# Sliding-window attention and a mixture of experts: the last expert's tiles fetch and turn the next tiles' x as all others do

## The chip, the cores and the metric

The kernel runs on one core of one Trainium2 chip. A core has TensorE (PE in the profile; its weight loads are listed as PEld), VectorE (DVE), ScalarE (ACT), GpSimd (POOL) and SyncE (SP), and 16 DMA engines which move data between HBM and the on-chip memory (SBUF, 128 partitions). TensorE writes its results to PSUM, which is divided into banks. The metric is the device time of one execution in microseconds; of several runs the median is given.

## The reference

What is computed are two layers, one after the other. The first is causal attention over a sliding window of 64 positions, for 8 batches, 8 heads, 576 positions and heads of 64. Its result is 4608 tokens of 512 numbers. The second is a mixture of 8 experts in which every token goes to one expert:

```python
logits = x @ w_gate                      # 4608 x 8
expert_idx = np.argmax(logits, axis=1)
probs = softmax(logits); gate_w = probs[token, expert_idx]
for e in range(E):                       # E = 8; the tokens of expert e
    h = np.maximum(x_sorted[lo:hi] @ w1[e], 0.0)      # 512 -> 1024
    y_sorted[lo:hi] = h @ w2[e]                       # 1024 -> 512
out = gate_w[:, None] * y                # back in the order of the tokens
```

How many tokens an expert gets depends on the data. With the reference's inputs the numbers are 669, 400, 748, 505, 592, 390, 566 and 738 for the experts 0 to 7. Everything is float32.

## The kernel before, in words

The first part of the program computes attention and the gate logits, scales every token by its gate weight and stores it as a row of x_dram in HBM (4608 rows, and row 4608, which holds zeros). Two tiles of expert 0 are begun here already. This takes a little over 300 us of the profile and the change doesn't touch its code.

The second part works on **tiles** of 256 slots (TB = 256, in C = 2 halves of 128). The experts' tiles are numbered one after the other; a table perm_i gives for each slot the token in it, or 4608 if the slot is empty. It has a column of 128 slots for each half tile, with columns for two halves ahead of tile 0, so that `slots(a)` in the tile numbered t is the tile t - 1 + a: `slots(0)` is the tile before, and `slots(3)` the second tile after t. The numbers run on from one expert to the next, and past the last tile the table holds empty slots only.

A tile is computed by body (L479). In order of the program it does this:

- finish() (L425) adds up the last part of the tile before, on DVE, and scatter (L291) writes that tile's rows to the output with two indirect DMAs issued from POOL.
- Where the tile is full, hidden (L336) computes h = relu(x w1) and output (L393) computes h w2. Both use a product with seven block multiplications in place of eight, so that sums and differences of blocks have to be formed: of the weights on POOL, of x and of the results on DVE. The order of all instructions on each engine is the order in which the program gives them.
- While TensorE works on this tile, the next tile's x is made ready. Its 256 rows lie in xg. turned_blocks (L310) turns them into xn with 16 DVE instructions, which are called in small groups between the other DVE work of the tile (`some(blocks, n)`); keep_turned (L325) copies xn to xq on ACT; sums_x (L329) forms four differences on DVE. The last two stand in output between the third and the fourth of its block products.
- When xg has been turned, gather (L272) fetches the x of the second tile after into xg: a small copy of the offsets and two indirect DMAs of 128 rows each, all on POOL.

If no more than 160 slots of an expert's last tile are used, half_tile (L436) computes it instead of hidden and output, in the plain form; it turns, gathers and sums in the same way.

The tiles of an expert are run by expert (L1063), one and more (L1070 to L1090). The numbers of tiles are known only when the kernel runs, so more nests branches: for each n up to KT - 1 = 2 there is one piece of code for a full tile and one for a half tile. All that is written once for each expert, since the weights' buffers change with e (w1s[e % 2] and so on, loaded by SP one expert ahead). If an expert has more than KT = 3 tiles, any_number (L1092) runs instead of all this; it is a loop over tiles without any overlap. It needs a small table, tiles_of.

In the last expert, one leaves something out. The lines are these:

```python
ends = e == E - 1 and (n == KT - 1 or not full)
body(e, slots(0), None if ends or e == E - 1 and n == KT - 2 else slots(3), full, between, not ends)
```

The third argument of body is what to gather (None: nothing), and the last one, next_x, says whether the next tile's x is turned and summed. With ends, that is in the third tile of the last expert and in any half tile of it, neither is done. In its second tile, if it is full, x is turned but nothing is gathered. After the last tile the code at L1126 and L1127 runs finish() and scatter() once more.

Of the kernel before, what the change touches and what calls it, by code (L numbers as in the profile page):

```python
# [11 lines left out]
F32 = mybir.dt.float32  # L12
# [3 lines left out]
ALU = mybir.AluOpType  # L16
AX = mybir.AxisListType
# [7 lines left out]
def _ins(ap: bass.AP, axis: int, n: int) -> bass.AP:  # L25

    dims = [list(d) for d in ap.ap]
    dims.insert(axis, [0, n])
    return bass.AP(tensor=ap.tensor, offset=ap.offset, ap=dims)


def _inner(ap: bass.AP, n: int) -> bass.AP:
    return _ins(ap, len(ap.ap), n)
# [3 lines left out]
def kernel(  # L37
# [11 lines left out]
    P = nc.NUM_PARTITIONS  # L49
    B, H, S, D = q.shape  # L50
    NT, DM = out.shape
    E = moe_w_gate.shape[1]
# [15 lines left out]
    NTILE = (NT + TB - 1) // TB + E - 1 + NE  # L68
    NX = NTILE + 4
    NS = NX * C  # L70
    KT = 3
# [24 lines left out]
    expert_i = consts.tile([P, NTILE], I32, name="expert_i")  # L96
# [4 lines left out]
    V, G = nc.vector, nc.gpsimd  # L101
# [48 lines left out]
    def sums_w1(e):  # L150
        form(left_sums(G, s1s[e % NW], *w1q(e)))
# [4 lines left out]
    def load_w1(e):  # L156
        return nc.sync.dma_start(out=w1s[e % NW][:], in_=w1v[e])
# [10 lines left out]
    lane = consts.tile([P, P], BF16, name="lane")  # L168
# [9 lines left out]
    with tc.tile_pool(name="tmp", bufs=1) as tmp:  # L178
# [8 lines left out]
        for i in range(BG):  # L187
# [12 lines left out]
            out=before[:], in_=ones[:], pattern=[[1, P]], compare_op=ALU.is_gt, fill=0.0, base=0,  # L200
# [6 lines left out]
    nt, cum, start, chunk0 = (consts.tile([P, E], F32, name=n) for n in ("nt", "cum", "start", "chunk0"))  # L207
    rt = ctx.enter_context(tc.tile_pool(name="rt", bufs=1))
# [31 lines left out]
    v_m = Memory(consts.tile([P, 3 * 2 * BG * NV * 2 * VW], F32, name="v_m"))  # L240
# [27 lines left out]
    def form_all(parts):  # L268
        for _ in parts:
            pass  # L270
# [20 lines left out]
    def scatter(tokens):  # L291
        G.tensor_copy(out=at_s[:], in_=tokens)
        for c in reversed(range(C)):

            put = G.indirect_dma_start(  # L295
                out=out[:, :], out_offset=bass.IndirectOffsetOnAxis(ap=at_s[:, c : c + 1], axis=0),
                in_=ys[c], in_offset=None, bounds_check=NT - 1, oob_is_err=False,
            )
            tc.declare_no_dep(put.ins, group="puts", reason="every token has one slot, so no row is written twice")
            tc.add_to_no_dep_group("puts", put.ins)  # L300
# [9 lines left out]
    def turned_blocks():  # L310

        rows = xg_all.rearrange("p c (g b j) -> p c g b j", b=P // QD, j=QD)
        for a in range(P // QD):
            for b in range(P // QD):
                V.transpose(  # L315
                    out=xn[b * QD : (b + 1) * QD, :, :, a * QD : (a + 1) * QD].rearrange("p c g i -> p (c g) i"),
                    in_=rows[a * QD : (a + 1) * QD, :, :, b, :].rearrange("p c g j -> p (c g) j"),
                )
                yield
# [73 lines left out]
    def output(e, blocks=None, next_x=True):  # L393

        b11, b12, b21, b22 = w2q(e)
        t = s2s[e % NW]
        a11, a12, a21, a22 = hq[:, 0, 0], hq[:, 1, 0], hq[:, 0, 1], hq[:, 1, 1]
        form(left_sums(V, hs, a11, a12, a21, a22))
        if blocks is not None:
            form_all(blocks)  # L400
        product_y(yx, a11, b11)
        nc.scalar.copy(out=y1, in_=yx)
        yield
        product_y(yw, a22, t[:, 3])
        yield
        product_y(yx, a12, b21, start=False)
        if blocks is None:
            sums_x(tps)
        elif next_x:
            keep_turned()  # L410
            sums_x([xn[:, c] for c in range(C)])
        yield
        product_y(yy, hs[:, 1], t[:, 1])
        yield
        product_y(yy2, hs[:, 2], t[:, 2])
        plus(v1, yy, y1)
        plus(v3, yy2, v1)
        V.tensor_tensor(out=ys[1][:, lo_], in0=v3, in1=yw, op=ALU.subtract)
        yield
        product_y(yw2, hs[:, 0], t[:, 0])  # L420
        yield
        product_y(yx2, hs[:, 3], b22)
        yield

    def finish():  # L425

        plus(ys[1][:, hi_], yw2, v3)
        plus(v2, yw2, v1)
        plus(ys[0], yps[0], v02)
# [49 lines left out]
    def body(e, last, after, full, between=None, next_x=True):  # L479

        finish()
        scatter(perm_i[:, last])
        if between is not None:
            between()
        blocks = turned_blocks() if next_x else iter(())
        if not full:
            half_tile(e, blocks, after, next_x)
            return
        form_all(hidden(e, blocks))
        parts = output(e, blocks, next_x)  # L490
        next(parts)
        if after is not None:
            gather(perm_i[:, after])
        form_all(parts)
# [559 lines left out]
    with tc.manual_schedule():  # L1054
        load_w1(1)
        load_w2(1)
        def at(n):
            n = nc.s_assert_within(
                n, 0, NTILE - 1, skip_runtime_bounds_check_because="a tile with a token is one of the NTILE"
            )  # L1060
            return lambda ahead: bass.ds((n + ahead) * C, C)

        def expert(e):  # L1063

            fulls, tiles, first = regs[e]
            if 0 < e < E - 1:
                load_w1(e + 1)
                load_w2(e + 1)

            def one(n, full, between=None):  # L1070
                slots = at(first + n)
                ends = e == E - 1 and (n == KT - 1 or not full)
                body(e, slots(0), None if ends or e == E - 1 and n == KT - 2 else slots(3), full, between, not ends)

            def more(n, between=None):

                with tc.If(tiles > n) as some_left:  # L1077
                    with tc.If(fulls > n, preferred_fallthrough_block=False) as full:
                        one(n, True, between)
                        if n + 1 < KT:  # L1080
                            more(n + 1)
                    with full.Else():
                        one(n, False, between)
                if between is not None:
                    with some_left.Else():
                        between()

            if e:
                one(0, True, partial(sums_w2, e))
            more(1 if e else NE, partial(sums_w1, e + 1) if e + 1 < E else None)  # L1090

        def any_number():  # L1092

            tiles_of = rt.tile([P, E, NTILE], F32, name="tiles_of")
            V.tensor_tensor(
                out=tiles_of[:], in0=_inner(cum[:], NTILE), in1=_ins(lane[:, 0:NTILE], 1, E), op=ALU.is_le
            )
            with nc.allow_low_precision("integers"):
                V.tensor_reduce(out=expert_i[:], in_=tiles_of[:].rearrange("p e t -> p t e"), axis=AX.X, op=ALU.add)
            _, (tiles,) = nc.values_load_multi_w_load_instructions(  # L1100
                places_i[0:1, E : E + 1], min_val=0, max_val=NTILE,
                skip_runtime_bounds_check_because="a sum of numbers of tiles, at most NTILE for any tokens",
            )
            with tc.For_i(NE, tiles) as i:
                _, (e,) = nc.values_load_multi_w_load_instructions(
                    expert_i[0:1, bass.ds(i, 1)], engines=(mybir.EngineType.SP,), min_val=0, max_val=E - 1,
                    skip_runtime_bounds_check_because="a tile that is numbered belongs to an expert",
                )
                for w, view in ((w1s[0], w1v), (w2s[0], w2v)):
                    nc.sync.dma_start(out=w[:], in_=view[bass.ds(e, 1)].rearrange("o p n d -> (o p) n d"))  # L1110
                sums_w1(0)
                sums_w2(0)
                slots = at(i)
                gather(perm_i[:, slots(1)])
                form_all(turned_blocks())
                keep_turned()
                sums_x([xn[:, c] for c in range(C)])
                form_all(hidden(0))
                form_all(output(0, iter(()), False))
                finish()  # L1120
                scatter(perm_i[:, slots(1)])

        with tc.If(most < KT + 1) as few:  # L1123
            for e in range(E):
                expert(e)
            finish()  # L1126
            scatter(perm_i[:, bass.ds(end * C, C)])  # L1127
        with few.Else():
            finish()
            scatter(perm_i[:, NE * C : (NE + 1) * C])  # L1130
            any_number()
# [28 lines left out]
```

## Time and profile before

| what | value |
|---|---|
| median of 3 runs | 722.04 us (720.9 to 725.24) |
| the profiled execution | 726.15 us, of which the span is 724.4 us |
| granted TensorE clock, mean | 0.989 |
| TensorE busy | 689.7 us, 95% of the span |
| DVE busy | 497.8 us, 69% |
| POOL busy | 350.7 us, 48% |
| ACT busy | 258.5 us, 36% |
| the last expert's three tiles begin | at 638.95, 663.54 and 688.13 us |
| TensorE's last work ends | at 713.1 us |
| the last scatter is issued | at 714.11 us, for 0.98 us |

The span is the time from the first to the last instruction that the profile holds. Engines are named as above. In a group, `out<-in` are the program's names for what is written and read, with the line of the kernel ahead; a helper's line stands for all its callers. What stands in brackets at the end of a row of the timeline is the time for which the engine was idle before it and what it waited for. In windows, the count in brackets is that of the instructions which ran in the stretch, wholly or in part, and the last three numbers are the TensorE clock, the share of the DMA engines and GB/s.

### The profile page before, as it was taken

Reading aid. Unit: us, or ns where it says so; the run is one execution under the profiler, and the core shown is the slowest. Engines: PE = TensorE matmul, PEld = TensorE weight load, DVE = VectorE, ACT = ScalarE, POOL = GpSimd, SP = SyncE. Lnnn points to the kernel's source line nnn. Section 1 sums busy time; section 2 is a strip of 40 time slices with the busy share of each in tenths; the row PEclk is TensorE's granted clock in tenths of the full one; section 3 lists DMA queues with packets and bytes.
Section 4 is the critical chain, followed back from the end, with each engine's and each line's share of the span. In section 5 each row is a group of like instructions: output and inputs, shape, how many; then the busy total and the mean of one; then the engine's idle time right before and its main releaser. Section 6 shows DMA issues by size and latency. Waiting matters only on the chain. (4 is left out here: it accounts for less than half of the span.)

```text
span 724.4 us, 17946 instructions
## 1 busy us (share of the span) xinstructions
PE 689.7 (95%) x6882; PEld 607.1 (84%) x6882; DVE 497.8 (69%) x1636; ACT 258.5 (36%) x653; POOL 350.7 (48%) x360
## 2 busy tenths in 40 slices
PE   5999999999879999999999999999999999999993
PEld 3887788888768898797999999899889799889993
DVE  3575898898965858675866686677766677666731
ACT  4787788888754211111211221112111111111110
POOL 4213748459375025937462356445274745272011
PEclk9999999999999999999999999999999999999997
DMA  8998898789361382715211531440261620111000
GB/s 159 219 195 186 176 188 230 168 188 235 106 194 47 121 291 81 258 59 202 102 38 60 161 133 57 154 170 30 88 243 59 242 69 30 61 37 61 2 30 28
DMA packets 137289, 93.37 MB, mean 129 GB/s; under 512 B 117009, under 2 KB 117009, under 8 KB 137171
## 3 DMA queue, kind: packets, MB, share of 16 engines
q1 hardware_dynamic: 127858, 62.16, 32.5%
q0 software_dynamic: 8736, 27.53, 11.7%
q10 hardware_dynamic: 576, 2.10, 0.9%
q8 instruction: 74, 1.21, 0.7%
q14 instruction: 45, 0.36, 0.2%
HBM read 72.89 MB, written 20.45 MB: 129 GB/s over the span
## 5 line engine op out<-in xcount | busy, mean ns | idle before, releaser
L315 DVE STREAM_TRANSPOSE v_m<-qk_m 32x256 f32<-32x256 f32 x304 | 132.4, 435 | 9.0 <-DMA qk_m<-x_dram,at_g 3.4
L344 PE MATMUL bank<-qk_m,s 128*128 128x128 f32 x1024 | 122.5, 275 | 1.0 <-DVE qk_m L365 1.0
L344 PEld LDWEIGHTS bank<-qk_m,s 128*128 128x128 f32 x1024 | 118.3, 192 | 1.2 <-issue 1.2
L275 POOL DMA_INDIRECT qk_m<-x_dram,at_g x38 | 41.0, 1080 | 142.4 <-DVE v_m L315 114.0
L651 ACT ACTIVATE pr<-pr,mx 128x128 f32<-128x128 f32 x288 | 89.7, 391 | 36.3 <-DVE mx L641 36.3
L344 PE MATMUL bank<-qk_m,w 128*128 128x128 f32 x768 | 93.8, 275 | 1.0 <-PEq L1077 0.9
L344 PEld LDWEIGHTS bank<-qk_m,w 128*128 128x128 f32 x768 | 90.6, 192 | 4.6 <-issue 4.2
L641 DVE CUSTOM_DVE_ANT_0 pr<-bank,mask 128x128 f32<-128x128 f32 x288 | 64.4, 286 | 30.7 <-PE bank L628 28.1
L295 POOL DMA_INDIRECT out_dram<-v_m,at_s x42 | 42.5, 1012 | 87.7 <-DVE v_m L384 85.1
L384 DVE TENSOR_TENSOR v_m<-bank,v_m 128x256 f32<-128x256 f32 (+1 forms) x95 | 43.8, 480 | 45.0 <-PE bank L388 30.1
L569 POOL COPY v_m<-v_m 64x520 f32<-64x520 f32 x32 | 19.8, 619 | 73.1 <-DMA v_m<-in_v_dram 72.5
L140 POOL TENSOR_TENSOR s<-w 128x1024 f32<-128x1024 f32 x22 | 52.2, 2372 | 0.0
L674 PEld LDWEIGHTS bank<-v_m,pT 128*64 128x64 f32 x1152 | 41.3, 141 | 12.0 <-DVE xs L688 5.8
L674 PE MATMUL bank<-v_m,pT 128*64 128x65 f32 x1152 | 47.9, 232 | 2.9 <-DVE xs L688 2.8
L388 PE MATMUL bank<-qkT_m,v_m 128*128 128x256 f32 x216 | 48.3, 379 | 0.0
L351 ACT COPY qk_m<-bank 128x512 f32<-128x512 f32 x16 | 9.4, 587 | 108.8 <-PE bank L344 63.2
L628 PE MATMUL bank<-qkT_m 64*64 64x128 f32 x1152 | 45.9, 290 | 0.1
L388 PEld LDWEIGHTS bank<-qkT_m,v_m 128*128 128x128 f32 x216 | 41.0, 190 | 5.5
L595 PE MATMUL bank<-ident,qk_m 128*128 128x128 f32 x256 | 37.0, 288 | 8.9 <-DMA qk_m<-in_q_dram 7.7
L444 PEld LDWEIGHTS bank<-qk_m,w 128*128 128x128 f32 x320 | 43.9, 190 | 0.9 <-issue 0.7
L444 PE MATMUL bank<-qk_m,w 128*128 128x160 f32 x320 | 44.4, 299 | 0.4 <-ACT qk_m L327 0.4
L659 PE MATMUL bank<-ident,pr 128*128 128x128 f32 x288 | 43.1, 287 | 0.0
(174 smaller groups left out, 1231.1 us busy)
## 6 DMA issues: line engine op xcount, KB each, us to landing
w<-in_moe_w_dram SPq DMA_DIRECT2D x11, 2048.0 KB, 10.0
qk_m<-in_q_dram SPq DMA_DIRECT2D x72, 128.0 KB, 3.8
qk_m<-in_k_dram SPq DMA_DIRECT2D x72, 128.0 KB, 3.7
v_m<-in_v_dram SPq DMA_DIRECT2D x64, 128.0 KB, 3.9
qk_m<-in_moe_w_dram SPq DMA_DIRECT2D x3, 2048.0 KB, 10.4
x_dram<-xs POOLq DMA_DIRECT2D x6, 512.0 KB
x_dram<-xs POOLq DMA_DIRECT2D x3, 768.0 KB
w<-in_moe_w_dram ACTq DMA_DIRECT2D x4, 512.0 KB, 4.3
```

The source lines that it names most:

```text
L140: op()
L295: put = G.indirect_dma_start(out=out[:, :], out_offset=bass.IndirectOffsetOnAxis(ap=at_s[:, c : c + 1], axis=0), in_=ys[c], in_offset=None ...
L315: V.transpose(out=xn[b * QD : (b + 1) * QD, :, :, a * QD : (a + 1) * QD].rearrange("p c g i -> p (c g) i"), in_=rows[a * QD : (a + 1) * QD ...
L344: nc.tensor.matmul(acc[:, f, :], lhsT=a[:, g, f * P : (f + 1) * P], rhs=b[:, g, :], start=(first and f == 0 and g == 0), stop=(g == HG - 1 ...
L384: plus = lambda out, a, b: V.tensor_tensor(out=out, in0=a, in1=b, op=ALU.add)
L388: nc.tensor.matmul(acc, lhsT=a[:, f, :], rhs=b[:, f, :], start=(start and f == 0), stop=(stop and f == HF - 1), skip_group_check=True,)
L444: nc.tensor.matmul(acc[:, i], lhsT=w1[:, g, f * P : (f + 1) * P], rhs=xq[:, g].rearrange("p c s -> p (c s)")[:, 0:HALF], start=(i + g == 0 ...
L628: nc.tensor.matmul(out_, lhsT=qT[rows, t, a * WINDOW : (a + 1) * WINDOW], rhs=rhs, start=True, stop=True, skip_group_check=True,)
L641: V.tensor_tensor_reduce(out=prs[h][:, m, :], in0=scs[h][:, m, :], in1=mask[:, m0 + m, :], scale=-scale, scalar=-2 * MASKED, op0=ALU.add, ...
L651: nc.scalar.activation(out=y, in_=y, func=AF.Exp, scale=-1.0, bias=mx[:, h, m : m + 1])
L659: nc.tensor.transpose(out=tr[:, m, :], in_=prs[h][:, m, :], identity=ident[:])
L674: nc.tensor.matmul(px[a * D : (a + 1) * D, h, m, :], lhsT=pTs[h][:, m, a * D : (a + 1) * D], rhs=vt[:, h, :], start=True, stop=True, skip_ ...
```

## The change

The last expert has no exception any more: each of its tiles, full or half, turns and sums the next tile's x and gathers that of the second tile after. Past the last tile these are empty slots, so that the gathers read row 4608 of x_dram. Beside that, the table tiles_of of any_number is placed in a part of v_m that is free there, and no longer gets memory of its own in the pool rt.

```diff
             def one(n, full, between=None):
                 slots = at(first + n)
-                ends = e == E - 1 and (n == KT - 1 or not full)
-                body(e, slots(0), None if ends or e == E - 1 and n == KT - 2 else slots(3), full, between, not ends)
+                body(e, slots(0), slots(3), full, between)
...
         def any_number():
 
-            tiles_of = rt.tile([P, E, NTILE], F32, name="tiles_of")
+            tiles_of = v_m(2080, E, NTILE)
             V.tensor_tensor(
-                out=tiles_of[:], in0=_inner(cum[:], NTILE), in1=_ins(lane[:, 0:NTILE], 1, E), op=ALU.is_le
+                out=tiles_of, in0=_inner(cum[:], NTILE), in1=_ins(lane[:, 0:NTILE], 1, E), op=ALU.is_le
             )
             with nc.allow_low_precision("integers"):
-                V.tensor_reduce(out=expert_i[:], in_=tiles_of[:].rearrange("p e t -> p t e"), axis=AX.X, op=ALU.add)
+                V.tensor_reduce(out=expert_i[:], in_=tiles_of.rearrange("p e t -> p t e"), axis=AX.X, op=ALU.add)
```

## The prediction

> **What bounds the kernel now.** I read the page's busy shares first, then the busy time of each engine in windows cut at the tiles of the last expert, then the instructions in order of time at the end of those tiles, and last what follows the final matmul. From the page:
>
> ```profile
> span 724.4 us, 17946 instructions
> ...
> PE 689.7 (95%) x6882; PEld 607.1 (84%) x6882; DVE 497.8 (69%) x1636; ACT 258.5 (36%) x653; POOL 350.7 (48%) x360
> ```
>
> TensorE is busy 95% of the span; DVE and POOL have room. The change concerns only the last expert (e = 7). With the reference's data it has 738 tokens, 256 + 256 + 226; the last rest is above 160, so all three tiles (n = 0, 1, 2) are full ones. Cut where each tile's L344 begins (the third window where the last TensorE work ends):
>
> ```profile
> core 0: us, PE busy (x) PEld busy (x) DVE busy (x) ACT busy (x) POOL busy (x), PEclk, DMA share, GB/s
> 638.95:663.54 24.59, 24.59 (x169) 22.96 (x167) 17.07 (x35) 4.58 (x8) 13.01 (x10) 1.00 0.09 28
> 663.54:688.13 24.59, 24.59 (x169) 23.15 (x168) 17.07 (x35) 4.58 (x8) 2.24 (x4) 1.00 0.07 24
> 688.13:713.10 24.97, 24.97 (x170) 23.15 (x168) 8.76 (x15) 3.45 (x6) 2.49 (x4) 1.00 0.06 23
> ```
>
> This table carries the forecast. Tile 0 does everything: it turns the next tile's x, forms its sums and fetches the tile after. Tile 1 turns and sums but fetches nothing (POOL 2.24 us). Tile 2 does neither (DVE 8.76 us in place of 17.07). TensorE is busy for the whole of each, and the tiles take the same time: the third window is longer only because it runs to the end of the last work, not to a next tile's start. The same reading at the ends, tile 0 and then tile 2:
>
> ```profile
> 657.79 1.14 ACT L327 COPY qk_m<-v_m 128x512 f32<-128x512 f32 x2 [3.77 <-DVE v_m L315]
> 658.43 1.22 DVE L333 TENSOR_TENSOR qk_m<-v_m,qk_m 128x256 f32<-128x256 f32 x3 [0.74 <-ACT qk_m L327]
> 658.49 1.26 POOL L275 DMA_INDIRECT qk_m<-x_dram,at_g  x1 [7.57 <-DVE v_m L315]
> ...
> 659.91 0.42 DVE L384 TENSOR_TENSOR v_m<-bank,v_m 128x256 f32<-128x256 f32 x1
> 660.05 0.97 POOL L275 DMA_INDIRECT qk_m<-x_dram,at_g  x1 [0.30 <-issue]
> 660.50 0.42 DVE L384 TENSOR_TENSOR v_m<-bank,v_m 128x256 f32<-128x256 f32 x1 [0.18 <-PE bank L388]
> ...
> 662.23 0.76 DVE L384 TENSOR_TENSOR v_m<-bank,v_m 128x256 f32<-128x256 f32 x2 [0.85 <-PE bank L388]
> 663.47 1.02 POOL L295 DMA_INDIRECT out_dram<-v_m,at_s  x1 [2.25 <-DVE v_m L384]
> ```
>
> ```profile
> 708.03 0.42 DVE L384 TENSOR_TENSOR v_m<-bank,v_m 128x256 f32<-128x256 f32 x1 [2.97 <-PE bank L388]
> 709.69 0.42 DVE L384 TENSOR_TENSOR v_m<-bank,v_m 128x256 f32<-128x256 f32 x1 [1.23 <-PE bank L388]
> ...
> 712.68 0.98 POOL L295 DMA_INDIRECT out_dram<-v_m,at_s  x1 [19.92 <-DVE v_m L384]
> ...
> 714.11 0.98 POOL L295 DMA_INDIRECT out_dram<-v_m,at_s  x1 [0.45 <-POOLq L1123]
> ```
>
> Counted from the tile's start (638.95 and 688.13), v1's add starts at 20.96 us with the extra work and 19.90 without; v3's add, which waits for TensorE in both, at 21.55 and 21.56; the scatter at 24.52 and 24.55. The extra work costs 1.06 us on v1 and is gone one instruction later. DVE's spare time behind it is 0.18 us before v3 and 0.85 us before the adds of finish(), 1.03 us together.
>
> [...]tile 0's two gathers end on POOL at 661.02 us, their packets run on to about 663.2 us (below). [...]the trace has both on one queue, q0. [...]
>
> **The change part by part.** *Tile 2 turns x and sums it* (next_x is always true). Added on DVE: 16 transposes at 435 ns (L315) = 6.97 us, 4 subtractions at 0.42 us (L333) = 1.7 us. Added on ACT: 2 copies (L327), 1.14 us. The windows count the same: 35 - 15 = 20 instructions on DVE (busy 17.07 - 8.76 = 8.3 us) and 8 - 6 = 2 on ACT. Cover: tile 0 and tile 1 have the identical sequence in the identical place and end alike, so the cost on the path is 0. Were the cover gone, it would be up to 6.97 + 1.7 + 1.1 = 9.8 us. No instruction of the PE is added. Behind the ACT copies nothing is queued in this tile but L402, which is already done.
>
> *Tiles 1 and 2 also gather.* Each adds on POOL a copy of 0.19 us and two indirect DMAs of 1.26 and 0.97 us with 0.3 us between, and 512 KB of transfer. The gather waits for the 16th transpose; queued behind it on POOL are the copy of at_s and the two scatters, which wait for finish() anyway. In tile 0 that copy ends at 661.22 us and the scatter then waits 2.25 us for DVE: so 0 here as well, with 2.25 us in hand. SP gets no new instruction.
>
> *What the added gathers fetch.* slots(3) of tile 1 and 2 are tiles 21 and 22 of 21, with no token: all 256 offsets are the zero row 4608 of x_dram. Tile 2's transposes need tile 1's gather; it starts at 683.1 us by tile 0's pattern and lands some 6 us later, before the first transposes, due at 4.66 us into the tile, 692.8 us. Tile 2's own gather is wanted by nobody but stands ahead of the final scatter on q0. Nothing shows a gather of nothing but zero rows, but expert 6's rest has 54 tokens, so its second half is 128 zero rows: gathered from 591.67 us. The same stretches (4.7 to 5.4 us after the gather's start) of that one and of tile 0's full one:
>
> ```profile
> 596.37:597.07 0.70, 0.70 (x6) 0.62 (x5) 0.00 (x0) 0.00 (x0) 0.42 (x1) 1.00 0.26 94
> ```
>
> ```profile
> 663.19:663.89 0.70, 0.70 (x6) 0.62 (x5) 0.00 (x0) 0.00 (x0) 0.42 (x1) 1.00 0.03 12
> ```
>
> 128 equal rows end up to 0.7 us later; 256 by that 1.4 us. Started at 688.13 + 19.54 = 707.67 us, the gather's packets then end between 712.4 (+4.7) and 713.8 us (+6.1). The scatter's first half moves its data from 713.5 us, its second from 715.5 us. Bounds for the final scatter: 0, and 0.3 us for its first half alone, which is not the last. I take 0.
>
> *The end.* What remains after the last scatter is a wait on POOL:
>
> ```profile
> L1155 POOLq DRAIN  x3: 46/113/9387, 714.1 to 724.1; - x3
> ```
>
> It runs from 714.1 to 723.5 us, though data stop at 716.5 us. The trace does not show what it is made of. POOL issues 102 DMAs in this run (38 + 42 + 4 + 12 + 6); if the wait were all for them it is 0.09 us each and 4 more cost 0.4 us; if it is fixed, 0. A gain is excluded: nothing that it could wait for goes away. I take 0.4 us.
>
> *tiles_of moves into v_m.* It is used in any_number alone, which does not run. Its 8 x 27 x 4 = 864 bytes a partition leave the pool rt, so what is opened later (xsp, att, wp with w1_1, s1_1, w2_1, s2_1) lies 864 bytes lower: w1_1 at 161344 in place of 162208. [...]all w1 loads land within 8.3 to 10.3 us; L344 takes 275 ns on either buffer. I take 0 and keep +-3 us.
>
> Sum: 0 + 0 + 0 + 0.4 + 0. Against the profiled execution's 726.15 us (span 724.4 and 1.75 around it) that is 726.6; it lies 4.1 us above the median 722.04, and what is added does not scale with that, so 722.4 us.
>
> **The rivals.** *(A) The final scatter is held up by the gather of zero rows*, which ends slower than now. Place: q0 after 712.7 us. It decides once the gather's data last past 713.5 us, 5.8 us after its start; beyond that every us counts nearly whole. If 256 equal rows queued on one another so that the gather took 13 to 14 us, the end moves by 8 us: 730. For it: no trace of a gather with both halves empty, and a scatter once waited for a gather to land (0.4 us, at 622 us). Against: 128 zero rows cost 0.7 us. *(B) The cover fails in the last tile*: more than 1.03 us late on DVE and the rest, 8.65 - 1.03 = 7.6 us, is on the path, 729.7. Against: tiles 0 and 1. *(C) The 864 bytes matter* somewhere in the attention part, where DMA is at nine tenths: 3 us either way, 719 or 725; more than 7 us is conceivable for 300 us of work but nothing shows it. *(D) The change doesn't do what it says*: if the last tile were a half one its cover would be L470; with 226 tokens it is not.
>
> **How the numbers follow.** Likeliest (no visible change, 722.4, own range 720.2 to 725.6 from the spread of the runs, 720.9 to 725.24): 0.80. A: 0.11, of it 0.07 by over 1%. B: 0.03. C: 0.06, of it 0.03 faster by over 1%, 0.01 slower by over 1%. One per cent, 7.2 us, is about what a measurement of this kernel can tell from no change. Faster 0.03, same 0.86, slower 0.11. The range takes the likeliest whole and the near parts of A and C: 719.8 to 728.
>
> **What would show it.** Right: tile 2's window holds 16 L315 and 4 L333 more, DVE near 17 us, and still some 24.6 us to the scatter; four more L275, the last near 709.2 us; the final scatters no later than 24.6 and 26.0 us into the tile; POOL's drain within 0.5 us of 9.4. A shows as q0 packets without pause past 713.5 us, B as L384 waiting for nothing before v3, C as other durations before 640 us. I am wrong if the drain depends on the gathers in a way that 0.09 us each does not cover, or if the attention part moves.

## The result

The changed kernel takes 719.12 us (median of 20 runs, 716.17 to 722.6) against 722.57 us before (20 runs beside them, 720.11 to 726.53). The ratio, worked out from all these runs and not from the two medians, is 0.9946, with a 95% interval of 0.9932 to 0.9960: faster by 2.9 to 4.9 us. I had forecast 722.4 us and a range from 719.8. The profiled execution took 719.24 us, its span is 717.5 us.

The windows of the last expert's tiles after, cut as before at L344:

```profile
core 0: us, PE busy (x) PEld busy (x) DVE busy (x) ACT busy (x) POOL busy (x), PEclk, DMA share, GB/s
636.18:660.77 24.59, 24.59 (x168) 22.96 (x167) 17.08 (x35) 4.59 (x8) 13.00 (x10) 1.00 0.11 27
660.77:685.36 24.59, 24.59 (x169) 23.15 (x168) 17.07 (x35) 4.58 (x8) 4.63 (x7) 1.00 0.15 44
685.36:710.33 24.97, 24.97 (x170) 23.15 (x168) 17.07 (x35) 4.59 (x8) 4.98 (x7) 1.00 0.15 46
```

All three tiles now do the whole of the work (DVE 17.07 us in tile 2, where it was 8.76), and they are as long as they were, to the hundredth. So neither a gain nor a loss lies in them. Tile 0 begins 2.8 us earlier than in the profile of before. The code up to there is the same but for where some buffers lie, and in e4 and e9 below, which differ from the kernel before only behind that point, the first final scatter starts at 711.59 and 714.43 us, as far apart; I don't count it.

The end of the timeline after, from the last turning on:

```profile
704.26 1.14 ACT L327 COPY qk_m<-v_m 128x512 f32<-128x512 f32 x2 [3.82 <-DVE v_m L315]
704.91 1.22 DVE L333 TENSOR_TENSOR qk_m<-v_m,qk_m 128x256 f32<-128x256 f32 x3 [0.74 <-ACT qk_m L327]
704.96 1.25 POOL L275 DMA_INDIRECT qk_m<-x_dram,at_g  x1 [17.02 <-DVE v_m L315]
706.05 0.42 DVE L333 TENSOR_TENSOR qk_m<-qk_m,v_m 128x256 f32<-128x256 f32 x1
706.38 0.96 DVE L384 TENSOR_TENSOR v_m<-bank,v_m 128x256 f32<-128x256 f32 x2
706.52 0.98 POOL L275 DMA_INDIRECT qk_m<-x_dram,at_g  x1 [0.30 <-issue]
...
709.95 1.02 POOL L295 DMA_INDIRECT out_dram<-v_m,at_s  x1 [2.25 <-DVE v_m L384]
710.37 0.69 DVE L384 TENSOR_TENSOR v_m<-bank,v_m 128x512 f32<-128x512 f32 x1 [0.92 <-PE bank L388]
712.91 1.01 POOL L295 DMA_INDIRECT out_dram<-v_m,at_s  x1 [1.94 <-POOLq L1122]
```

Each tile's rows go out with two scatters, so that the last tile has a first and a second final scatter. The first starts 24.59 us into its tile, where it was 24.55. The second starts 1.85 us after DVE's last add has ended (710.37 + 0.69 = 711.06 us). Before, that add was this line of the timeline, and the scatter at 714.11 us followed 0.28 us after its end, 713.83 us:

```profile
713.14 0.69 DVE L384 TENSOR_TENSOR v_m<-bank,v_m 128x512 f32<-128x512 f32 x1 [0.92 <-PE bank L388]
```

So the second final scatter lost 1.57 us. The gain is in what comes last, the wait of POOL's queue at the end of the program (shortest, median and longest of three in ns, then the starts of the first and the last); the line to compare is that of L1155 before, with 9387 ns:

```profile
L1154 POOLq DRAIN  x3: 46/113/3132, 712.9 to 717.2; - x3
```

3.13 us in place of 9.39: 6.26 us less. Not all of that is won. The trace also has SP waiting for the DMA of out_dram, that is for the scatters' data to land; that wait ends at 717.0 us before and at 715.7 us after, and SP's first DRAIN starts 0.6 us later in both. In before that DRAIN was 5.9 us ahead of the end of POOL's wait (714.1 + 9.39 = 723.5 us); after, it is 0.3 us behind it (712.9 + 3.13 = 716.0 us), so that POOL's wait no longer ends last. Before, then after:

```profile
L1155 SPq DRAIN  x3: 7/7/13, 717.6 to 723.8; - x3
```

```profile
L1154 SPq DRAIN  x3: 7/7/13, 716.3 to 716.6; - x3
```

From the end of DVE's last add to the end of the span there were 10.57 us (724.4 - 713.83) and are 6.44 us (717.5 - 711.06). The difference, 4.13 us, is the 6.26 us without the 1.57 us of the second scatter and without some 0.6 us at the very end, where SP is now last. It lies inside the measured interval of 2.9 to 4.9 us. I call this stretch the **tail** and compare all kernels by it, since it is free of what the attention part does from run to run.

### The profile page after: what moved, and what is told of

The parts are those of the page before. It is cut to its first block, busy times and chain, and to the rows that moved or that the text cites. A ratio compares the mean times of both kernels' runs of the same rounds, so it can differ in the third digit from the quotient of the medians.

```text
span 717.5 us, 17980 instructions
## 1 busy us (share of the span) xinstructions
PE 687.2 (96%) x6882; PEld 606.0 (84%) x6882; DVE 505.1 (70%) x1656; ACT 259.9 (36%) x655; POOL 355.2 (50%) x366
## 5 line engine op out<-in xcount | busy, mean ns | idle before, releaser
L315 DVE STREAM_TRANSPOSE v_m<-qk_m 32x256 f32<-32x256 f32 x320 | 139.3, 435 | 8.6 <-DMA qk_m<-x_dram,at_g 2.7
L275 POOL DMA_INDIRECT qk_m<-x_dram,at_g x42 | 45.4, 1081 | 176.1 <-DVE v_m L315 147.1
L344 PE MATMUL bank<-qk_m,s 128*128 128x128 f32 x1024 | 122.5, 275 | 0.6 <-DVE qk_m L365 0.6
L344 PEld LDWEIGHTS bank<-qk_m,s 128*128 128x128 f32 x1024 | 118.3, 192 | 0.8 <-issue 0.8
L344 PE MATMUL bank<-qk_m,w 128*128 128x128 f32 x768 | 93.8, 275 | 0.8 <-DVE v_m L384 0.8
L344 PEld LDWEIGHTS bank<-qk_m,w 128*128 128x128 f32 x768 | 90.6, 192 | 4.3 <-issue 4.0
L327 ACT COPY qk_m<-v_m 128x512 f32<-128x512 f32 x40 | 22.7, 615 | 62.4 <-DVE v_m L315 62.4
L628 PE MATMUL bank<-qkT_m 64*64 64x128 f32 x1152 | 44.2, 284 | 0.1
```

Of the source, the lines that this page charges most:

```text
L275: G.indirect_dma_start(out=xg[c], out_offset=None, in_=x_dram[:, :], in_offset=bass.IndirectOffsetOnAxis(ap=at_g[:, c : c + 1], axis=0),)
L315: V.transpose(out=xn[b * QD : (b + 1) * QD, :, :, a * QD : (a + 1) * QD].rearrange("p c g i -> p (c g) i"), in_=rows[a * QD : (a + 1) * QD ...
L344: nc.tensor.matmul(acc[:, f, :], lhsT=a[:, g, f * P : (f + 1) * P], rhs=b[:, g, :], start=(first and f == 0 and g == 0), stop=(g == HG - 1 ...
L628: nc.tensor.matmul(out_, lhsT=qT[rows, t, a * WINDOW : (a + 1) * WINDOW], rhs=rhs, start=True, stop=True, skip_group_check=True,)
```

## The experiments

The wait in question is one instruction, DRAIN, in POOL's own queue; the trace names nothing that releases it. The theories were these. *Theory 1*: POOL had been idle for 20 us before the final scatters, and the added gathers keep it awake. *Rival 2*, later *C*: the number of DMAs that POOL has issued decides, 102 before and 106 after. *Rival 3*: the 864 bytes of memory. *Rival 4*: DVE's and ACT's work in the last tile. *L*: where POOL's code lies. *N*: a gather near the end. *D*: not only the number of POOL's DMAs but also their size, counted here in rows. All tails and last waits, of one profiled execution each:

| kernel | POOL's DMAs | their rows | last wait, us | tail, us |
|---|---|---|---|---|
| before | 102 | 14208 | 9.39 | 10.57 |
| e1, memory only | 102 | 14208 | 9.38 | 10.54 |
| e4, turning without gather | 102 | 14208 | 9.38 | 10.56 |
| e5, a POOL copy before the end | 102 | 14208 | 9.39 | 10.56 |
| e9, code shifted | 102 | 14208 | 9.38 | 10.82 |
| e8, two more DMAs early | 104 | 14464 | 9.55 | 10.70 |
| e13, four tiny DMAs early | 106 | 14212 | 9.70 | 10.81 |
| the change | 106 | 14720 | 3.13 | 6.44 |
| e2, exceptions only | 106 | 14720 | 3.13 | 6.45 |
| e3, gather without turning | 106 | 14720 | 3.13 | 6.49 |
| e6, four more DMAs early | 106 | 14720 | 3.13 | 6.07 |
| e12, six small DMAs early | 108 | 14976 | 3.60 | 4.86 |
| e14, sixty small DMAs early | 162 | 21888 | 6.36 | 7.76 |
| e10, stores moved to SP | 84 | 10752 | 8.09 | 9.28 |
| e11, and half the scatters | 63 | 8064 | 6.18 | 7.82 |

The rows are counted from the program, not measured: 128 for every indirect DMA, and for a load or a store the rows that it moves. Before, that makes 84 indirect DMAs x 128 = 10752, and 3456 for the 18 stores (6 x 256 + 3 x 384 + 3 x 128 + 6 x 64).

### The parts of the change

**e1**, tiles_of moved, and nothing else:

```diff
-            tiles_of = rt.tile([P, E, NTILE], F32, name="tiles_of")
+            tiles_of = v_m(2080, E, NTILE)
```

> Only tiles_of moves into v_m; the last expert keeps its exceptions. Theory 1 (the time was won in the last wait on POOL, because POOL has work shortly before the final scatter): no change, ratio 0.998 to 1.002, and the wait on POOL after the final scatter stays near 9.4 us. Rival 2 (the number of DMAs that POOL issues decides where some upkeep of its falls): no change either, 102 DMAs as before. Rival 3 (864 bytes lower in memory speed up the attention part): the whole gain is here, ratio about 0.995, with tile 0 of the last expert beginning some 3 us earlier.

Measured: ratio 1.0003 (0.9983 to 1.0024), wait 9.38 us. No gain shows, and the tail is that of before; rival 3 falls.

**e2**, the rest of the change:

```diff
-                ends = e == E - 1 and (n == KT - 1 or not full)
-                body(e, slots(0), None if ends or e == E - 1 and n == KT - 2 else slots(3), full, between, not ends)
+                body(e, slots(0), slots(3), full, between)
```

> Only the exceptions of the last expert go; tiles_of keeps its own memory. Theory 1 and rival 2: the whole gain, ratio about 0.995, wait on POOL after the final scatter near 3 us. Rival 3: no change, ratio 1.0; wait as it may be, tile 0 of the last expert begins no earlier than before.

Measured: ratio 0.9963 (0.9946 to 0.998), wait 3.13 us, tail 6.45 us. By the tail, the whole gain is here.

**e3**, the gathers without the turning in tile 2:

```diff
-                body(e, slots(0), None if ends or e == E - 1 and n == KT - 2 else slots(3), full, between, not ends)
+                body(e, slots(0), slots(3), full, between, not ends)
```

> The second and third tile of the last expert gather (106 DMAs on POOL as in the change) but the third turns and sums nothing, so that its gather waits for no DVE work and runs at the tile's start, some 20 us ahead of the final scatter. Theory 1: POOL is idle again for nearly 20 us before the final scatter, the wait on POOL is near 9 us, ratio near 1.0. Rival 2: same number of DMAs as in the change, wait near 3 us, ratio 0.995. Rival 4 (DVE's or ACT's work in the last tile decides): wait 9 us, ratio 1.0.

Measured: ratio 0.9961 (0.9943 to 0.9978), wait 3.13 us. The end of its timeline on POOL:

```profile
687.17 1.00 POOL L275 DMA_INDIRECT qk_m<-x_dram,at_g  x1 [0.27 <-issue]
688.48 0.98 POOL L275 DMA_INDIRECT qk_m<-x_dram,at_g  x1 [0.31 <-DMA out_dram<-v_m,at_s]
689.44 0.21 POOL L292 COPY at_s<-perm_i 128x2 int32 x1
708.89 1.02 POOL L295 DMA_INDIRECT out_dram<-v_m,at_s  x1 [19.24 <-DVE v_m L384]
711.86 1.01 POOL L295 DMA_INDIRECT out_dram<-v_m,at_s  x1 [1.94 <-POOLq L1123]
```

POOL does nothing for 19.24 us ahead of the final scatter, and yet the end is that of the change, with the 1.94 us before the second scatter too. Theory 1, my first, falls here; so does any part of the turning in tile 2. Since the gathers ran 20 us before, their data can't be what holds the second scatter back either.

**e4**, the turning without the gathers:

```diff
-                body(e, slots(0), None if ends or e == E - 1 and n == KT - 2 else slots(3), full, between, not ends)
+                body(e, slots(0), None if ends or e == E - 1 and n == KT - 2 else slots(3), full, between)
```

> The third tile of the last expert turns and sums (its x is what tile 0 had left in place, unused after), but the second and third tile gather nothing: POOL's instructions are those of before. Theory 1 and rival 2: no change, ratio 1.0, wait on POOL 9.4 us. Rival 4 (the DVE and ACT work in the last tile decides): ratio 0.995, wait near 3 us.

Measured: ratio 1.0 (0.9981 to 1.002), and the last wait is that of before:

```profile
L1155 POOLq DRAIN  x3: 46/113/9382, 713.0 to 723.0; - x3
```

The 16 transposes, 4 differences and 2 copies cost nothing, as forecast, and gain nothing. Rival 4 falls. What is left is the gathers: their number, their place, or their code.

### Number, place or code

**e5**, a POOL copy that waits for the last tile's v1:

```diff
             for e in range(E):
                 expert(e)
+            G.tensor_copy(out=low[:, 0:C], in_=v1[:, 0:C])
             finish()
```

> The kernel before, with one small POOL copy (128 x 2) that waits for v1 of the last tile, so that POOL computes some 4 us ahead of the final scatter; the DMAs are those of before. Theory C (the number of DMAs that POOL has issued decides where the wait falls): wait on POOL after the final scatter near 9.4 us, second final scatter 0.3 us after its data are ready. The fallen theory 1 (idle POOL): wait near 3 us. Theory L (where POOL's instructions lie and how many it runs decides): either, since one instruction is added.

Measured: wait 9.39 us. Work on POOL 4 us ahead of the final scatter changes nothing, which confirms the fall of theory 1.

**e6**, four more DMAs, far from the end; **e8**, two more:

```diff
         gather(perm_i[:, 4 * C : 5 * C])
+        gather(perm_i[:, 4 * C : 5 * C])
+        gather(perm_i[:, 4 * C : 5 * C])    # e6 only
```

> The kernel before, with two more gathers (four indirect DMAs of 128 rows, the same rows as the one ahead of them) some 440 us before the end, and the last expert's exceptions kept: 106 DMAs on POOL as in the change. Theory C: the end looks as in the change, wait near 3.1 us and the second final scatter held back by 1.5 us; span some 4 us shorter than before, unless the early gathers delay tile 2. Theory N (what counts is a gather close to the end, after the second tile's scatter): wait near 9.4 us, no gain.

> The kernel before, with one more gather (two indirect DMAs) some 440 us before the end: 104 DMAs on POOL. Theory C: the end differs from before; if it is a limit that is passed at a certain number of DMAs, the wait lies at 9.4 or at 3.1 us and the stall has moved by two DMAs, perhaps to a place where nothing waits for it. Theory N: wait near 9.4 us.

e6's timeline on POOL and its last wait:

```profile
723.67 0.98 POOL L295 DMA_INDIRECT out_dram<-v_m,at_s  x1 [20.09 <-DVE v_m L384]
726.59 0.99 POOL L295 DMA_INDIRECT out_dram<-v_m,at_s  x1 [1.93 <-POOLq L1125]
```

```profile
L1157 POOLq DRAIN  x3: 46/113/3130, 726.6 to 730.7; - x3
```

DMAs added 440 us earlier have the same effect on the end as gathers in the last tile. Theory N falls. (The span, 730.9 us, is not shorter, since the first final scatter already starts 11 us later than before; that delay lies ahead of the tail and is not explained here.) With two more, e8, the wait is 0.16 us longer than before, not shorter:

```profile
L1156 POOLq DRAIN  x3: 46/113/9547, 716.7 to 726.8; - x3
```

Something is passed between 104 and 106 DMAs.

**e9**, 27 instructions in a branch that doesn't run:

```diff
                 slots = at(first + n)
+                if e == E - 1 and n == 1 and not full:
+                    for _ in range(27):
+                        G.memset(low[:, 0:1], 0.0)
```

> The kernel before, with 27 memsets on POOL in a branch of the last expert that does not run (its half tile for n = 1): POOL's code from the second tile on lies as far behind as in the change, what runs is as before. Theory L: wait near 3 us and the second final scatter held back by 1.5 us, span some 4 us shorter. Theories C and N: wait near 9.4 us, no gain.

Measured: wait 9.38 us. Theory L falls.

### Number of DMAs, or of rows

By the count of rows, the 105th DMA of the change ends at 14592 and the 106th at 14720, and the 106th is the scatter that is held back (POOL is idle for 1.94 us ahead of it, where before has 0.45). Theory D takes it that the rows decide, and not the number of DMAs; why they should is not shown by any trace. The next five runs test that.

**e13**, 106 DMAs, but of one row:

```diff
         regs, end, most = loads()
+        for i in range(4):
+            G.dma_start(out=low[0:1, 6 * i : 6 * i + 6], in_=moe_w1[0, 0:1, 6 * i : 6 * i + 6])
```

> The kernel before, with four loads of one row of 24 bytes issued by POOL some 440 us before the end: 106 DMAs as in the change[...]. Theory D: [...]the end is that of before: wait 9.4 to 9.5 us, second final scatter not held back. Theory C: the end of the change: wait 3.1 us, second final scatter held back by 1.5 us.

Its last two scatters and its last wait:

```profile
711.94 0.98 POOL L295 DMA_INDIRECT out_dram<-v_m,at_s  x1 [20.09 <-DVE v_m L384]
713.37 0.98 POOL L295 DMA_INDIRECT out_dram<-v_m,at_s  x1 [0.45 <-POOLq L1125]
```

```profile
L1157 POOLq DRAIN  x3: 46/115/9703, 713.4 to 723.7; - x3
```

The second scatter is not held back and the wait is long. 106 DMAs alone don't do it; theory C falls as to the point at which the end changes. This is the one run that tells the number of DMAs from their size. But the wait grew by 0.32 us for four tiny DMAs, 0.08 us each, as much as by each of the 128-row gathers in e8: its length goes by DMAs.

**e12**, six loads of 128 rows, so that the 106th DMA is the second scatter at the start of the last tile:

```diff
         regs, end, most = loads()
+        for i in range(6):
+            G.dma_start(out=low[:, 6 * i : 6 * i + 6], in_=moe_w1[0, 0:P, 6 * i : 6 * i + 6])
```

> The kernel before, with its exceptions for the last expert, and six small loads (128 rows of 24 bytes, to a place that is free) issued by POOL some 440 us before the end: 108 DMAs[...]. Theory D: [...]the final scatters are the 107th and 108th, the second is not held back, the wait is near 3.1 us. So the end gains 6.2 us on before and 1.5 us on the change: ratio to before 0.990 to 0.993, a little better than the change. Theory N (a gather near the end): ratio 1.0.

Its timeline on POOL from the last tile's start:

```profile
685.06 0.98 POOL L295 DMA_INDIRECT out_dram<-v_m,at_s  x1 [19.68 <-DVE v_m L384]
687.99 0.99 POOL L295 DMA_INDIRECT out_dram<-v_m,at_s  x1 [1.95 <-issue]
690.97 0.18 POOL L292 COPY at_s<-perm_i 128x2 int32 x1 [1.98 <-DMA out_dram<-v_m,at_s]
709.71 0.98 POOL L295 DMA_INDIRECT out_dram<-v_m,at_s  x1 [18.55 <-DVE v_m L384]
711.12 0.98 POOL L295 DMA_INDIRECT out_dram<-v_m,at_s  x1 [0.44 <-POOLq L1125]
```

The stall of 1.5 us (1.95 us where the kernel before has 0.49) is still at the 106th DMA, but that is now the scatter at the tile's start, for which nothing waits. The final one follows at once, the last wait is 3.60 us, where 3.1 was expected, and the tail 4.86 us, the shortest of all. Measured: medians of 717.29 us against 721.84, ratio over all runs 0.9945 (0.9915 to 0.9974), where 0.990 to 0.993 was expected. By its tail it should be 1.6 us better than the change; the intervals can't tell the two apart, so that this part isn't shown by the times.

**e10**, the stores of x_dram issued from SP, and **e11**, which also leaves out the second half of every scatter:

```diff
-                        do(5 + m * 2 // 3, partial(store, bg, m // ST, G))
+                        do(5 + m * 2 // 3, partial(store, bg, m // ST, nc.sync))
...
-                    do(3 + m // ST, partial(store, bg, m // ST, G))
+                    do(3 + m // ST, partial(store, bg, m // ST, nc.sync))
...
-        for c in reversed(range(C)):
+        for c in (0,):                      # e11 only
```

> The kernel before, with the 18 stores of x_dram that POOL issues moved to SP: 84 DMAs on POOL in place of 102[...]. Theory D (the last wait on POOL grows[...]): [...]7.2 us[...], 7.9 us[...]. Theory C (the number of DMAs, past 105 it is short): 7.9 to 8.3 us if it grows with DMAs, 9.4 us if it doesn't.

> As e10, and of every tile only the first half is scattered (the rows of the second half are left out of the output): 63 DMAs[...]. Theory D: 5.5 us[...], 6.7 us[...]. Theory C: 6.2 to 7.0 us, or 9.4 us.

Measured:

```profile
L1155 POOLq DRAIN  x3: 46/113/8093, 707.7 to 716.4; - x3
```

```profile
L1155 POOLq DRAIN  x3: 46/113/6178, 709.2 to 716.0; - x3
```

Theory D's 7.2 to 7.9 us for e10, with 3456 rows fewer than before, and 5.5 to 6.7 us for e11, with 6144 fewer, are estimates; by rows they follow from 0.63 ns a row (e8: 0.16 us for 256) and 0.44 ns (9.38 - 3.13 us over 14208). The 8.09 us of e10 lie in theory C's range and above D's; the 6.18 us of e11 lie in D's range and just below C's. So neither range settles it, but the two steps together do: without 18 stores the wait is 1.29 us shorter, 0.072 us each; without 21 scatters 1.91 us more, 0.091 us each. By rows, 3456 and 2688 of them, these would be 0.37 and 0.71 ns, nearly a factor of two apart, so DMAs are the better measure of the wait's length here too. Neither run comes near the 106th DMA, and in neither is a scatter held back by 1.5 us.

**e14**, sixty loads, so that some 56 DMAs follow the 106th:

```diff
         regs, end, most = loads()
+        spare = of[:].rearrange("p e j -> p (e j)")
+        for i in range(60):
+            G.dma_start(out=spare[:, 4 * i : 4 * i + 4], in_=moe_w1[0, 0:P, 4 * i : 4 * i + 4])
```

> The kernel before, with 60 small loads (128 rows of 16 bytes, to a place that is free) issued by POOL in tile 1: 162 DMAs[...]. The 106th DMA[...] is now among the early ones, and some 56 DMAs come after it. Theory D1 (the last wait grows by 0.08 us for each DMA[...], from about 1.2 us, and is at least as long as the last scatter takes to land, 3.1 to 3.6 us): 1.2 + 56 x 0.08 = 5.7 us. Theory D2 ([...]the wait stays short, however many DMAs follow): 3.1 to 3.6 us. Theory D3 (it grows with all DMAs of the program after all): over 13 us. The span itself is longer by what the loads take on POOL and says nothing.

The last wait, and on the timeline of POOL the 105th and the 106th DMA:

```profile
L1158 POOLq DRAIN  x3: 46/109/6361, 735.3 to 742.2; - x3
```

```profile
384.39 1.03 POOL L295 DMA_INDIRECT out_dram<-v_m,at_s  x1 [2.26 <-DVE v_m L384]
387.27 1.01 POOL L295 DMA_INDIRECT out_dram<-v_m,at_s  x1 [1.85 <-issue]
```

The 106th is held back again (1.85 us where 0.43 is usual), 350 us before the end. The wait, 6.36 us, is neither short for good (D2) nor grows with all 162 DMAs (D3, over 13 us): it is what a count that starts again at the 106th gives (D1). It is 0.7 us longer than D1's sum of 5.7, so that the straight line is only a rough one, and this is one run.

## Why the prediction was wrong

**What held.** *Tile 2 turns x and sums it*, at no cost: the windows are equal, and e4 has it alone at ratio 1.0. *The gathers cost no engine anything* before the end: the first final scatter stands 24.59 us into its tile. *What the gathers fetch*: in tile 2 the gather's packets ended between 710.5 and 711 us, 5.5 to 6 us after its start, within the 4.7 to 6.1 I had worked out from the half-empty tile. The data were gone before the final scatter's began at 711.5 us, so rival A did not come about: the second scatter is held back as much in e3 and e6, whose gathers ran 20 and 440 us earlier. *tiles_of*: 0, shown by e1.

**What failed** is the term for the wait at the end, and in it one sentence: "A gain is excluded: nothing that it could wait for goes away." I had the right lead: 9.39 us over 102 DMAs, 0.09 us each, "if the wait were all for them". The runs give 0.07 to 0.09 us. But I let the four new DMAs add to the sum, 0.4 us, as if the count ran through the program. The runs show that it does not (e14, with 162 DMAs, waits 6.36 us and not over 13): as I read them it starts again at a certain point, and in the change that point is the last DMA, the 106th. By the count of rows, before ended at 14208 and after at 14720. In place of + 0.4 us, the wait lost 6.26 us. The prediction had named this as a way to be wrong, a drain that depends on the gathers otherwise than by 0.09 us each, but gave it no share of its chances.

A second term failed the other way. For the final scatter I had looked only at the gather's data, and taken 0. The first final scatter kept its place, but the second started 27.55 us into the tile (712.91 - 685.36), where I had named 26.0 us as the latest: 1.57 us lost at the same 106th DMA. With the 0.6 us at which SP is now last, 4.1 us are left of the gain. The range ended 0.7 us above the measured median because of the first bound: the cost of an unknown wait was kept from falling below nothing for a reason that was not one.

These points remain open. The traces don't show what POOL does in the wait, only that its length follows the DMAs since the start or since that point. The waits of 3.13 us and 3.60 us can't be used for that count, since they end 0.3 and 0.1 us ahead of SP's first DRAIN, which follows SP's wait for the data, and may be no more than the landing of the last scatter. What happens where the count starts again is not shown either; the runs place that point after 14592 and up to 14720 rows as I count them, and e13 alone shows that it is not the number of DMAs. What the traces count of POOL's DMA queue does not fit: up to and with the 106th DMA it had moved 566 packets for each engine and 28.6 MB in the change, 386 packets and 14.1 MB in e14 (worked out from its 10656 packets and 27.66 MB, less 80 packets for each of the 56 later DMAs and 13.5 MB for their rows), and the stall is there in both, with 1.94 and 1.85 us. Nor do packets tell the loads of e13, which don't bring the stall, from those of e12: 32 for each load in both. And the tail of 4.1 us comes from profiled executions; the timed gain agrees with it (2.9 to 4.9 us), no more.

## What to carry to other kernels

A wait whose content the profile doesn't show must be left open on both sides: price it by all that it might count, and ask where that count begins. Where GpSimd issues many DMAs, compare the wait at the program's end between kernels before looking for a gain elsewhere; here it moved by 6 us while no tile took a different time. Where a program ends just short of the point at which such a count starts again (here, as I read the runs, after 14592 and up to 14720 rows), a few small DMAs issued earlier, at a quiet place, may do as much as this change: in e12 six of them gave a ratio of 0.9945.

## What the runs showed that I had not expected

- The last wait on POOL was 9.38 to 9.39 us in five kernels with 102 DMAs, grew by 0.08 us for each DMA that e8 and e13 added, and fell to 3.13 us in the four kernels whose last DMA is the one with which the rows pass 14592.
- That DMA, always the 106th, is held back by 1.4 to 1.5 us: in the change, e2, e3, e6, e12 and e14 alike.
- Moving that DMA away from the end (e12) makes the tail 4.86 us; the change has 6.44 and the kernel before 10.57.
- A wait can be shortened by more than it is worth: POOL's lost 6.26 us, but in the change SP, which waits for the last data, reaches its first DRAIN 0.3 us after POOL's wait has ended.
